# Relu kept in PSUM: convolution and gate read it there, and the order of the work is drawn anew

## The chip, the cores and the metric

One NeuronCore of a Trainium2 chip runs the whole program. The metric is the device time of one execution in microseconds, the median of a few runs. The engines are called TensorE (PE), VectorE (DVE), ScalarE (ACT), GpSimd (POOL) and SyncE (SP); the last issues nearly all DMAs.

## What is computed

Eight sequences of 576 positions go through causal attention with eight heads of 64, with a bias from a running sum, and then through a feed-forward block with a convolution of three taps over the positions:

```python
scores = where(causal, -1e9, q @ k.T / 8 + min(-(cum[i] - cum[j]), 0))
x = softmax(scores) @ v                       # 8 x 576 x 512
h = maximum(x @ w_in, 0)                      # 8 x 576 x 1024
conv_out[s] = cw[0]*h[s-1] + cw[1]*h[s] + cw[2]*h[s+1]
out = (h * sigmoid(conv_out)) @ w_out         # 8 x 576 x 512
```

All inputs and the output are fp32. The kernel keeps near fp32 accuracy by splitting operands into a high and a low part (`fp32r`) and summing three products.

## The kernel before

**Tiling.** The attention runs over 32 pairs of heads (`pair(p)`). For a pair TensorE forms scores (task `sh`, line L1106) of which VectorE takes the maximum of each row (`mx`, L1143, with the row sums `rw` added for pairs from 7 on), then the scores again transposed (`sc`, L1230), of which ScalarE takes a sigmoid in place of the exponential (L1247), then sums and the product with v (`sum` L1333, `pv` L1281). The block after it runs over eight batches, two halves of the positions (320 and 256 columns) and four pairs of 128 features: 64 groups, `moe_h(b, hf, fp)`. A group is 48 products into one PSUM pair (task `h`, L1446), the Relu (L1467, ScalarE), the middle tap (L1481 on ScalarE or L1483 on VectorE), two outer taps for each of its two feature blocks (L1496, VectorE), a sigmoid (L1510, ScalarE), the product with h (L1516, VectorE), and the split into `u` (L1525, L1530). The output products `o` (L1595) follow, and their copies (L1629) and stores.

**PSUM.** It is used as four tiles `ps0` to `ps3` of two banks each, here called pairs. A task that allocates one (`psb()`) keeps it until the last task that uses it is done. The Relu reads the pair and writes `ht` in SBUF, and the pair is free after it; the taps and the product read `ht`. A token `qh` lets two groups be between their first product and their Relu.

**The order.** A planner (`Sched.play`) plays the whole program once, while the program is built, with a fixed duration for each task, and writes the instructions out in the order in which its play started them. Each engine then takes its own instructions strictly in that order and waits where data or a buffer is missing. Among ready tasks the planner takes the one with the lowest due time, which is a formula plus a shift from the table `DUE`. It counts a DMA as landed `LAND` us (`LAND0` in the first 100 us) after its bytes have passed. Tasks marked as needing the SBUF port that VectorE shares with GpSimd (a third entry `True` in the options) are not started on both engines at once, and where one was made to wait, a dependency is added between them. Where TensorE would stand for more than 0.6 us (in the first 100 us, at all), and a PSUM pair is free, it is given a product of the mask that nobody reads (`stay_awake`, L1661). The row sums `rw` of a pair of heads come by one DMA (576 KB, L1055) into a single buffer.

Of the kernel before, what the change touches and what calls it, by code (L numbers as in the profile page):

```python
# [17 lines left out]
ALU = mybir.AluOpType  # L18
# [33 lines left out]
LAND = 0.85  # L52
NEAR = 0.2
LANES, RATE0, EARLY, LAND0 = 8, 300e3, 100.0, 1.2
# [41 lines left out]
    "pads":  # L96
        "0 -12.85 1 -220.76 2 -41.24",
    "ind":
# [396 lines left out]
def kernel(  # L495
# [928 lines left out]
    def h_tag(b, hf, f):  # L1424
        return at(HP * (b + 1)) + LAG + hf * HT + f * HT / NF

    def moe_h(b, hf, fp):
        u, ht, ct = buf("u"), buf("ht"), buf("ct")
        hw = HW[hf]
        k0 = hw - 2 * P  # L1430
        tg = h_tag(b, hf, 2 * fp)
# [307 lines left out]
```

## Time and profile before

| | us |
|---|---|
| median of 3 runs | 764.38 (763.74 to 765.69) |
| the profiled execution | 767.12 |
| its span, first to last instruction | 765.4 |
| TensorE busy in it | 733.4 |
| VectorE, ScalarE, GpSimd busy | 543.9, 406.2, 283.0 |
| mean granted TensorE clock | 0.993 |

Matmuls overlap each other, so the start of one row to the start of the next tells more of TensorE's pace than the length of a row. A row of a time line joins alike instructions (x24), and the bracket behind it tells how long the engine stood before it and what ended that.

### The profile page before, as it was taken

Reading aid. Unit: us, or ns where it says so; the run is one execution under the profiler, and the core shown is the slowest. Engines: PE = TensorE matmul, PEld = TensorE weight load, DVE = VectorE, ACT = ScalarE, POOL = GpSimd, SP = SyncE. Lnnn points to the kernel's source line nnn. Section 1 sums busy time; section 2 is a strip of 40 time slices with the busy share of each in tenths; the row PEclk is TensorE's granted clock in tenths of the full one; section 3 lists DMA queues with packets and bytes.
Section 4 is the critical chain, followed back from the end, with each engine's and each line's share of the span. In section 5 each row is a group of like instructions: output and inputs, shape, how many; then the busy total and the mean of one; then the engine's idle time right before and its main releaser. Section 6 shows DMA issues by size and latency. Waiting matters only on the chain.

```text
span 765.4 us, 24336 instructions
## 1 busy us (share of the span) xinstructions
PE 733.4 (96%) x10066; PEld 620.0 (81%) x10066; DVE 543.9 (71%) x1438; ACT 406.2 (53%) x714; POOL 283.0 (37%) x403
## 2 busy tenths in 40 slices
PE   7999999989999999899999899999899999999999
PEld 5787888879887788777888689777787887888997
DVE  7899997664967678785578848767875795756642
ACT  6566655465645356454655535545565454734441
POOL 5646420324143512536344262344157426311000
PEclk9999999989999999999999999999999999999999
DMA  7667532242333322334122443233323421101001
GB/s 224 207 190 219 155 90 85 69 130 64 97 94 114 99 77 71 107 100 143 51 89 65 125 157 85 79 125 99 100 63 101 115 85 59 45 18 45 28 30 43
DMA packets 50089, 75.50 MB, mean 99 GB/s; under 512 B 13690, under 2 KB 26298, under 8 KB 49978
## 3 DMA queue, kind: packets, MB, share of 16 engines
q1 hardware_dynamic: 49960, 73.92, 32.0%
q8 instruction: 79, 1.29, 0.7%
q14 instruction: 32, 0.26, 0.1%
q10 hardware_dynamic: 18, 0.02, 0.0%
HBM read 63.53 MB, written 10.03 MB: 96 GB/s over the span
## 4 chain that ended last, share of the span: by engine, by line
PE 57%; DVE 16%; DMA 12%; POOL 6%; issue 6%; ACT 3%; SPq 1%; POOLq 0%; DVEq 0%; ACTq 0%
PE ps L1595 19%; PE ps L1446 18%; PE ps L1230 9%; PE ps L1281 6%; DVE ps L1143 5%; DMA rw<-cum_d 4%; DVE ct L1496 3%; DMA rb<-ri_d 3%; PE ps L1333 2%; PE ps L1106 2%; POOL ad L1296 2%; DMA raw<-qk 2%; DVE r L1143 1%; POOL rw L1064 1%; POOL pt L1258 1%
## 5 line engine op out<-in xcount | busy, mean ns | idle before, releaser
L1446 PE MATMUL ps<-x,wi 64*128 64x258 f32 (+1 forms) x3072 | 228.5, 297 | 4.0 <-DVE r L1143 2.1
L1446 PEld LDWEIGHTS ps<-x,wi 64*128 64x128 f32 x3072 | 214.2, 187 | 11.0 <-DVE r L1143 2.6
L1595 PE MATMUL ps<-wo,u 64*128 64x512 f32 x1536 | 193.3, 393 | 0.7
L1143 DVE CUSTOM_DVE_ANT_0 ps<-ps,rw 128x448 f32<-128x448 f32 (+4 forms) x250 | 109.6, 439 | 97.7 <-POOL rw L1064 38.8
L1595 PEld LDWEIGHTS ps<-wo,u 64*128 64x128 f32 x1536 | 140.3, 185 | 29.0 <-ACTq L811 2.5
L1247 ACT ACTIVATE pt<-ps,less 128x1024 f32<-128x1024 f32 (+1 forms) x128 | 116.2, 925 | 28.6 <-PE ps L1230 24.3
L1496 DVE SCALAR_TENSOR_TENSOR ct<-ht,cw_sb,ct 128x320 f32<-128x320 f32 (+3 forms) x256 | 123.6, 524 | 9.7 <-POOL u L1530 4.6
L1064 POOL TENSOR_SCALAR_AFFINE_SELECT rw<-rw 128x256 f32<-128x256 f32 (+1 forms) x125 | 48.2, 393 | 206.8 <-DVE ct L1496 79.7
L1230 PE MATMUL ps<-s 64*128 64x288 f32 (+4 forms) x1152 | 109.3, 303 | 7.4 <-ACT pt L1247 3.1
L1230 PEld LDWEIGHTS ps<-s 64*128 64x128 f32 (+1 forms) x1152 | 82.8, 181 | 14.1 <-ACT pt L1247 4.8
L1281 PE MATMUL ps<-pt,v 128*32 128x448 f32 (+4 forms) x1536 | 92.8, 388 | 0.0
L1258 POOL TENSOR_SCALAR_AFFINE_SELECT pt<-pt 128x256 f32<-128x256 f32 (+1 forms) x115 | 43.5, 397 | 108.9 <-DVE ct L1496 41.4
L1281 PEld LDWEIGHTS ps<-pt,v 128*32 128x32 f32 x1536 | 50.6, 110 | 39.8 <-issue 29.9
L1467 ACT ACTIVATE ht<-ps 128x642 f32<-128x642 f32 (+1 forms) x64 | 41.8, 652 | 64.5 <-PE ps L1446 64.2
L1510 ACT ACTIVATE ct<-ct 128x640 f32<-128x640 f32 (+1 forms) x64 | 43.7, 683 | 43.3 <-DVE ct L1496 39.9
L1106 PE MATMUL ps<-s 64*128 64x288 f32 (+4 forms) x384 | 50.1, 319 | 9.1 <-DVE r L1143 7.2
L1516 DVE TENSOR_TENSOR ct<-ct,ht 128x640 f32<-128x640 f32 (+1 forms) x64 | 48.4, 756 | 9.0 <-ACT ct L1510 7.2
L1525 ACT CAST u<-ct 128x512 fp32r<-128x512 f32 x56 | 34.6, 618 | 30.9 <-DVE ct L1516 30.3
L1230 PE MATMUL ps<-eq,ek 64*128 64x288 f32 (+1 forms) x360 | 50.6, 301 | 0.0
L1481 ACT ACTIVATE ct<-ht,cw_sb 128x320 f32<-128x320 f32 (+1 forms) x95 | 47.7, 531 | 2.4
L1106 PEld LDWEIGHTS ps<-s 64*128 64x128 f32 x384 | 33.4, 189 | 18.7 <-DVE r L1143 10.5
L1143 DVE DVE_READ_ACCUMULATOR2_ANT r<- 128x1 f32 x314 | 44.4, 141 | 0.0
(120 smaller groups left out, 933.5 us busy)
## 6 DMA issues: line engine op xcount, KB each, us to landing
raw<-qk SPq DMA_DIRECT2D x32, 576.0 KB
rw<-cum_d SPq DMA_DIRECT2D x25, 576.0 KB
v<-vp SPq DMA_DIRECT2D x32, 320.0 KB
rb<-ri_d SPq DMA_DIRECT2D x64, 144.0 KB
out<-ob SPq DMA_DIRECT2D x32, 256.0 KB
w<-w_in SPq DMA_DIRECT2D x8, 512.0 KB
ht<-w_out SPq DMA_DIRECT2D x8, 256.0 KB
w<-w_out SPq DMA_DIRECT2D x4, 512.0 KB
```

The source lines that it names most:

```text
L1064: nc.gpsimd.affine_select(out=RW_t[:, :, o : o + k], in_=RW_t[:, :, d : d + k], pattern=[[0, 2], [-1, k]], compare_op=ALU.is_ge, fill=NEG, ...
L1106: nc.tensor.matmul(dst[j], l, m, start=(k == 0), stop=(k == 1 or late))
L1143: nc.vector.tensor_tensor_reduce(out=bank(pb, j, o, o + c1 - c0), in0=bank(pb, j, o, o + c1 - c0), in1=add_, scale=1.0, scalar=acc if c0 e ...
L1230: nc.tensor.matmul(d, l, m, start=(k < 2), stop=(k >= len(steps) - 2 or (t == L and k < 2)), skip_group_check=t == L,)
L1247: nc.scalar.activation(PT[:, :, o : o + w], both(pb, 0, w), AF.Sigmoid, bias=less, scale=0.125,)
L1258: nc.gpsimd.affine_select(out=reg, in_=reg, pattern=[[0, 2], [1, dg]], compare_op=ALU.is_ge, fill=0.0, base=0, channel_multiplier=-1,)
L1281: nc.tensor.matmul(bank(pvs, n, o0, o0 + c1 - c0)[gs], vt[0:jt, t, gs], PT_t[g // 2][0:jt, O_T[t] + c0 : O_T[t] + c1], start=(t == 0), sto ...
L1446: mm = nc.tensor.matmul(bank(hb, i, 0, XW[hf]), wi[rows[j], k_ // 2, c, f * P : f * P + P], x[rows[j]], start=not turned and k == 0, stop= ...
L1481: nc.scalar.activation(o, src, AF.Copy, scale=w)
L1496: nc.vector.scalar_tensor_tensor(cc[:, lo:hi], h_[:, sh + lo : sh + hi], cw_sb[:, 3 * f + k : 3 * f + k + 1], cc[:, lo:hi], op0=ALU.mult, ...
L1516: nc.vector.tensor_tensor(cc, cc, H_t[ht.slot][:, :, hf : hf + hw], op=ALU.mult)
L1595: mm = nc.tensor.matmul(bank(pb2 if m else pb, m, 0, cw_), l, r, start=turned + fp + n == 0, stop=turned == 1 and fp == FP - 1 and n == le ...
```

## The change

Three things are changed. The Relu writes back into the PSUM pair that it reads; `ht` is no longer allocated by a group. The middle tap, the outer taps and the product with h read the pair; the pair and the token `qh` stay with the group until that product is done. The outer taps of a group wait for both of its middle taps. These tasks no longer carry the mark of the shared port, and their planned durations are those below. `LAND` goes from 0.85 to 1.3, `LAND0` from 1.2 to 1.425. And every shift in `DUE` is another number.

```diff
-LAND = 0.85
+LAND = 1.3
-LANES, RATE0, EARLY, LAND0 = 8, 300e3, 100.0, 1.2
+LANES, RATE0, EARLY, LAND0 = 8, 300e3, 100.0, 1.425
...
     "h":
-        "0.0 -27.58 0.1 14.39 1.0 28.37 1.1 73.88 2.0 51.44 2.1 91.75 3.0 -156.77 3.1 71.3 "
+        "0.0 -347.28 0.1 -5.08 1.0 -98.9 1.1 -51.12 2.0 -60.78 2.1 268.69 3.0 -326.95 "
...
-        u, ht, ct = buf("u"), buf("ht"), buf("ct")
+        u, ct = buf("u"), buf("ct")
...
             nc.scalar.activation(
-                H_t[ht.slot][:, :, 0 : hw + 1], both(hb, hf, hf + hw + 1), AF.Relu
+                both(hb, hf, hf + hw + 1), both(hb, hf, hf + hw + 1), AF.Relu
             )
...
-                     uses=[hb, ht, q])
+                     uses=[hb, q])
+        t_cs = []
...
-                src = H_t[ht.slot][:, i, hf : hf + hw]
+                src = bank(hb, i, 2 * hf, 2 * hf + hw)
...
-            t_c = add(f"ce{b}.{hf}.{f}", [("ACT", 0.29 + hw / 1.2e3), ("DVE", 0.21 + hw / 1.92e3, True, 2.0)],
-                      [t_relu, t_cw], h_tag(b, hf, f) + 0.1, center, uses=[ht, ct])
-
-            t_tap = t_c
+            t_c = add(f"ce{b}.{hf}.{f}", [("ACT", 0.29 + hw / 1.2e3), ("DVE", 0.2 + hw / 0.96e3, False, 3.0)],
+                      [t_relu, t_cw], h_tag(b, hf, f) + 0.1, center, uses=[hb, ct])
+            t_cs.append(t_c)
+
+        for i in range(2):
+            f = 2 * fp + i
+            t_tap = t_cs
...
-                    h_ = H_t[ht.slot][:, i, :]
+                    h_ = bank(hb, i, hf, hf + hw + 1)
...
-                t_tap = add(f"t{'ab'[k // 2]}{b}.{hf}.{f}", [("DVE", 0.205 + hw / 0.96e3, True)], [t_tap],
-                            h_tag(b, hf, f) + 0.1, tap, uses=[ht, ct])
+                t_tap = add(f"t{'ab'[k // 2]}{b}.{hf}.{f}", [("DVE", 0.215 + hw / 0.96e3)], t_tap,
+                            h_tag(b, hf, f) + 0.1, tap, uses=[hb, ct])
...
-                cc, cc, H_t[ht.slot][:, :, hf : hf + hw], op=ALU.mult
+                cc, cc, both(hb, 2 * hf, 2 * hf + hw), op=ALU.mult
...
-        t_m = add(f"mu{b}.{hf}.{fp}", [("DVE", c_tt(2 * hw), True)], [t_g], tg, mul, uses=[ct, ht])
+        t_m = add(f"mu{b}.{hf}.{fp}", [("DVE", c_tt(2 * hw) + 0.03)], [t_g], tg, mul, uses=[ct, hb, q])
```

TensorE's order before, in the first half of batch 5: two groups (`x0`, `wi`) take turns in `ps0` and `ps1`, and the sums of a pair of heads (`pt`, `onehot`) go into `ps0`.

```order
L1595 MATMUL ps3_67<-wo_75,u0_1768 128x512 x12
L1446 MATMUL ps0_64<-x0_89,wi_74 128x322 x24
L1446 MATMUL ps1_65<-x0_89,wi_74 128x322 x24
L1446 MATMUL ps0_64<-x0_89,wi_74 128x322 x24
L1446 MATMUL ps1_65<-x0_89,wi_74 128x322 x24
L1333 MATMUL ps0_64<-pt_88,onehot_70 32x128
```

Between the last product of the group in `ps0` and the next writer of `ps0` stand 24 products. TensorE's order after, in the same half batch: a group in `ps3`, the scores of the next pair (`s1`), a group of the second half (`x1`) in `ps0`, and the sums into `ps3`.

```order
L1448 MATMUL ps3_67<-x0_89,wi_74 128x322 x24
L1108 MATMUL ps2_66<-s1_79 128x448 x2
L1108 MATMUL ps2_66<-s1_79 128x64 x2
L1448 MATMUL ps3_67<-x0_89,wi_74 128x322 x24
L1108 MATMUL ps1_65<-s1_79 128x320 x2
L1108 MATMUL ps1_65<-s1_79 128x192 x2
L1448 MATMUL ps0_64<-x1_90,wi_74 128x258 x48
L1335 MATMUL ps3_67<-pt_88,onehot_70 32x128
```

Now four score products and 48 products of the next group stand between the last product into `ps3` and its next writer, and that writer needs the whole gate of the group to be done. VectorE's order before, at two groups of the same half batch (`ct0` and `ct1` are their results, `ISA` is a row maximum and the read of its result):

```order
L1483 TENSOR_SCALAR ct0_103<-ht0_100,cw_sb_73 128x320
L1496 SCALAR_TENSOR_TENSOR ct0_103<-ht0_100,cw_sb_73,ct0_103 128x319 x2
L1496 SCALAR_TENSOR_TENSOR ct0_103<-ht0_100,cw_sb_73,ct0_103 128x320 x2
L1496 SCALAR_TENSOR_TENSOR ct1_104<-ht1_101,cw_sb_73,ct1_104 128x319 x2
L1496 SCALAR_TENSOR_TENSOR ct1_104<-ht1_101,cw_sb_73,ct1_104 128x320
L1516 TENSOR_TENSOR ct0_103<-ct0_103,ht0_100 128x640
```

VectorE's order after, at the group in `ps3` of the fence above:

```order
L1523 TENSOR_TENSOR ct2_105<-ct2_105,ps0_64 128x640
L1486 TENSOR_SCALAR ct0_103<-ps3_67,cw_sb_73 128x320
L1502 SCALAR_TENSOR_TENSOR ct0_103<-ps3_67,cw_sb_73,ct0_103 128x319 x2
L1502 SCALAR_TENSOR_TENSOR ct0_103<-ps3_67,cw_sb_73,ct0_103 128x320 x2
L1145 ISA ps2_66,r0_94<-ps2_66,rw_84 128x64
L1145 ISA r0_94 128x1
```

The taps read `ps3` in place of `ht0`, and row maxima of the next scores stand between them and the group's product (L1523). Over the whole program the order of TensorE has 228 products of the mask in place of 242; VectorE has 52 middle taps in place of 33, and GpSimd 50 subtractions for x in place of 20.

## Rows read from the trace of the kernel before

**Rows 1.** The page's first part: busy us, share of the span, instructions.

```profile
PE 733.4 (96%) x10066; PEld 620.0 (81%) x10066; DVE 543.9 (71%) x1438; ACT 406.2 (53%) x714; POOL 283.0 (37%) x403
```

**Rows 2.** TensorE's groups by line: count, busy us, mean ns, idle before, releasers.

```profile
L1661 PE MATMUL ps<-mask 128*128 128x256 bf16 x242 | 33.1, 284 | 4.5 <-POOL mask L678 2.2 <-ACT ht L1467 1.8 <-DVE r L1143 0.5
```

**Rows 3.** TensorE's waits: who waited for whom, us in total, times, longest.

```profile
PE ps L1106 <- DVE r L1143: 7.2, 7, 2.7
...
PE ps L1446 <- ACT ht L1467: 1.2, 2, 0.7
```

**Rows 4.** TensorE's time line at 156 us: start, length, instructions, wait before.

```profile
156.41 0.80 PE L1106 MATMUL ps<-s 64*128 64x448 f32 x4 [2.70 <-DVE r L1143]
```

**Rows 5.** Two stretches: length, busy PE, PEld, DVE, ACT, POOL, clock, DMA.

```profile
145.00:165.00 20.00, 17.30 (x255) 14.89 (x255) 12.33 (x33) 11.20 (x19) 8.08 (x9) 0.83 0.35 110
310.00:322.00 12.00, 9.96 (x112) 8.83 (x108) 8.46 (x26) 3.85 (x9) 6.75 (x12) 0.86 0.41 138
```

**Rows 6.** VectorE's and GpSimd's time lines at 150 and at 314 us.

```profile
150.37 2.87 DVE L1496 SCALAR_TENSOR_TENSOR ct<-ht,cw_sb,ct 128x255 f32<-128x255 f32 x1 [2.61 <-POOL rw L1064]
...
150.31 2.65 POOL L992 TENSOR_TENSOR s<-raw,s 128x1152 fp32r<-128x1152 f32 x1
...
314.52 0.47 DVE L1143 CUSTOM_DVE_ANT_0 ps<-ps,rw 128x288 f32<-128x288 f32 x1
...
314.48 1.47 POOL L1411 TENSOR_TENSOR x<-rb,x 128x322 fp32r<-128x322 f32 x2
```

**Rows 7.** Time lines of SyncE, VectorE and TensorE around 313 us.

```profile
308.45 0.39 SPq L1055 DMA_DIRECT2D rw<-cum_d  x1
...
313.96 0.47 DVE L1143 CUSTOM_DVE_ANT_0 ps<-ps,rw 128x288 f32<-128x288 f32 x1 [1.89 <-DMA rw<-cum_d]
...
315.10 0.50 PE L1106 MATMUL ps<-s 64*128 64x448 f32 x4 [1.99 <-DVE r L1143]
```

**Rows 8.** TensorE's time line at the first scores.

```profile
7.68 2.69 PE L1661 MATMUL ps<-mask 128*128 128x256 bf16 x23
...
11.45 0.40 PE L1106 MATMUL ps<-ek,eb 64*128 64x288 f32 x2 [0.75 <-ACT ek L1039]
```

**Rows 9.** Groups by line and shape on ScalarE and VectorE; last, VectorE's time line.

```profile
L1467 ACT ACTIVATE ht<-ps 128x642 f32<-128x642 f32 x32 | 22.6, 707 | 38.5 <-PE ps L1446 38.3
L1467 ACT ACTIVATE ht<-ps 128x514 f32<-128x514 f32 x32 | 19.1, 598 | 26.0 <-PE ps L1446 25.8
L1481 ACT ACTIVATE ct<-ht,cw_sb 128x320 f32<-128x320 f32 x48 | 25.1, 557 | 1.3
L1481 ACT ACTIVATE ct<-ht,cw_sb 128x256 f32<-128x256 f32 x47 | 22.6, 505 | 1.1
L1510 ACT ACTIVATE ct<-ct 128x640 f32<-128x640 f32 x32 | 23.6, 737 | 15.6 <-DVE ct L1496 12.3 <-PE ps L1595 1.8 <-PE ps L1230 1.4
L1510 ACT ACTIVATE ct<-ct 128x512 f32<-128x512 f32 x32 | 20.1, 629 | 27.6 <-DVE ct L1496 27.6
...
L1516 DVE TENSOR_TENSOR ct<-ct,ht 128x640 f32<-128x640 f32 x32 | 26.3, 822 | 3.9 <-ACT ct L1510 3.3 <-POOL rw L1064 0.6
L1516 DVE TENSOR_TENSOR ct<-ct,ht 128x512 f32<-128x512 f32 x32 | 22.1, 689 | 5.1 <-ACT ct L1510 3.9 <-POOL pt L1258 0.7 <-POOL rw L1064 0.5
L1496 DVE SCALAR_TENSOR_TENSOR ct<-ht,cw_sb,ct 128x320 f32<-128x320 f32 x64 | 33.4, 545 | 0.1
L1496 DVE SCALAR_TENSOR_TENSOR ct<-ht,cw_sb,ct 128x256 f32<-128x256 f32 x64 | 29.1, 477 | 2.7 <-POOL u L1530 2.1 <-ACT ct L1481 0.2
L1143 DVE CUSTOM_DVE_ANT_0 ps<-ps,rw 128x320 f32<-128x320 f32 x50 | 24.9, 499 | 13.3 <-POOL rw L1064 11.0 <-PE ps L1106 1.5
...
140.67 1.67 DVE L1496 SCALAR_TENSOR_TENSOR ct<-ht,cw_sb,ct 128x256 f32<-128x256 f32 x4
```

**Rows 10.** TensorE's time line at 137 us: 48 products of h, and the next row.

```profile
137.41 3.11 PE L1446 MATMUL ps<-x,wi 64*128 64x258 f32 x48
140.32 0.59 PE L1230 MATMUL ps<-s 64*128 64x288 f32 x6
```

More of the change, by code (lines that the diff above doesn't have):

```diff
@@ L91 @@
     "x":
[4 rows of a table removed]
[4 rows of a table added]
     "pads":
-        "0 -12.85 1 -220.76 2 -41.24",
+        "0 -135.98 1 -136.71 2 -132.38",
     "ind":
[1 row of a table removed]
[1 row of a table added]
     "cw":
[1 row of a table removed]
[1 row of a table added]
     "wi":
[3 rows of a table removed]
[3 rows of a table added]
     "wo":
[6 rows of a table removed]
[6 rows of a table added]
     "qk":
[9 rows of a table removed]
[9 rows of a table added]
     "hi":
[4 rows of a table removed]
[4 rows of a table added]
     "lo":
[4 rows of a table removed]
[4 rows of a table added]
     "dr":
[4 rows of a table removed]
[4 rows of a table added]
     "dp":
[1 row of a table removed]
[1 row of a table added]
     "dq":
[1 row of a table removed]
[1 row of a table added]
     "eq":
[4 rows of a table removed]
[4 rows of a table added]
     "sh":
[4 rows of a table removed]
[4 rows of a table added]
     "tn":
[4 rows of a table removed]
[4 rows of a table added]
     "sc":
[4 rows of a table removed]
[4 rows of a table added]
     "pv":
[4 rows of a table removed]
[4 rows of a table added]
     "nm":
[4 rows of a table removed]
[4 rows of a table added]
     "fo":
[4 rows of a table removed]
[4 rows of a table added]
     "vn":
[4 rows of a table removed]
[4 rows of a table added]
     "rw":
[3 rows of a table removed]
[3 rows of a table added]
     "rk":
[12 rows of a table removed]
[14 rows of a table added]
 }
@@ L1459, in moe_h @@
                        [x_done[b * HP + c] for c in range(NC)] + [t_wi[2 * fp], t_wi[2 * fp + 1]],
-                       h_tag(b, hf, 2 * fp + i), h_mm(i), alloc=[hb, u, ht, ct, q] if i == 0 else [],
+                       h_tag(b, hf, 2 * fp + i), h_mm(i), alloc=[hb, u, ct, q] if i == 0 else [],
                        uses=xs + ([hb] if i else []), mode="r")
@@ L1500, in tap @@
                     )
-                t_tap = add(f"t{'ab'[k // 2]}{b}.{hf}.{f}", [("DVE", 0.205 + hw / 0.96e3, True)], [t_tap],
-                            h_tag(b, hf, f) + 0.1, tap, uses=[ht, ct])
-            taps.append(t_tap)
+                t_tap = add(f"t{'ab'[k // 2]}{b}.{hf}.{f}", [("DVE", 0.215 + hw / 0.96e3)], t_tap,
+                            h_tag(b, hf, f) + 0.1, tap, uses=[hb, ct])
+                t_tap = [t_tap]
+            taps += t_tap
         tg = h_tag(b, hf, 2 * fp + 1) + 0.2
```

162 rows, old and new, of the table DUE are left out of this document.

## The prediction

> **What bounds the kernel now.** I read the page's first part, then TensorE's groups by line, then TensorE's waits, then the time lines around the longest of them. TensorE is busy 733.4 of 765.4 us; no other engine is over 71% [rows 1]. So the time is TensorE's own work plus whatever it waits for. Of its busy time 33.1 us is no work: 242 products of the mask (L1661) that the planner puts where it expects TensorE to stand still, so that the clock stays up [rows 2]. Idle (765.4 - 733.4 = 32.0) and filler together are 65 us, and that is all this change can move, because it alters no real product. The longest single entry among the waits is 7.2 us for a score product (L1106) that needs a PSUM pair which VectorE's row maxima (L1143) still hold [rows 3].
>
> Two of these waits are long and cost twice. At 153.7 us TensorE stands 2.70 us [rows 4], and the granted clock over 145 to 165 us is 0.83; at 313 us it stands 1.99 us [rows 7], and the clock over 310 to 322 is 0.86 [rows 5]. Missing clock is 0.17 x 20 = 3.4 us and 0.14 x 12 = 1.7 us. I read the fall as the follower of a wait near 2 us.
>
> **The change part by part.** The two orders differ nearly everywhere, so I price kinds of waits. The profiled execution took 767.12 us (765.4 of them span), 2.7 more than the median 764.38; I take the sum as a difference and put it on the median.
>
> *Fillers after 100 us.* The order before has 70 fillers there ahead of its last run, the order after 32. A filler is worth 2.69 / 23 = 0.117 us [rows 8], so 38 fewer give **-4.4 us** if they stand for wait that is gone. They may not: a filler needs a free PSUM pair, and the change keeps pairs longer, so a wait can stand there unfilled. Taken -4.1, bounds -4.4 and 0.
>
> *Fillers ahead of the first scores.* 64 instead of 46. In the trace these run until the first score product at 10.4, and the bias product behind it then waits 0.75 us for the key rows until 11.45 us [rows 8]. 18 x 0.117 = 2.1 us more would move both to 12.4, 1.0 later than now. Bounds 0 and +1.0; the other fillers up to 100 us change by 3. Taken **+0.7**.
>
> *Taps and the gate product read PSUM.* Before, both their inputs are in SBUF. At 150.37 us one tap took 2.87 us, in step with a subtraction on GpSimd that took 2.65 [rows 6]; four such taps otherwise take 1.67 [rows 9]. The maxima behind that tap are what TensorE waited for at 153.7. A VectorE operation with one input in PSUM did not stretch beside such subtractions: 0.47 us at 314.52, while two of GpSimd's ran from 314.48 to 315.95 [rows 6]. So the taps stop colliding. The price is that place: at most 2.70 + 3.4 = 6.1 us, at least 0 if another wait is next there. Taken **-4.0**. The tap's own length changes little: with one input in PSUM, 320 columns took 0.499 us in the maxima against 0.545 in the taps [rows 9], so -0.05 to +0.05 each; 256 x 0.05 = 13 us on an engine that is idle 221 us is covered except inside the chain below. The middle tap loses more on VectorE: the order has 52 there instead of 33. What the planner moves from VectorE to GpSimd (30 of the 64 subtractions of x, 26 of u and us) goes to an engine that is 37% busy; I cost it at nothing.
>
> *The planner's landing time.* It rises from 0.85 to 1.3 us. The load of the row sums, issued at 308.45, let the maxima go at 313.96, 5.5 us on, and TensorE waited 1.99 us [rows 7]. A later planned landing puts other work in front. This kind is 1.99 + 1.7 of clock there and at most what is left of the entry of 7.2 us without its two long waits, 7.2 - 2.7 - 2.0 = 2.5: 6.2 us. Bounds -6.2 and 0; taken **-3.0**, since 0.45 us is a small part of 5.5.
>
> *The pair is held longer.* This is what the change adds. Before, the pair of an h group comes free when the Relu has been written to SBUF; after, only when the gate product has been formed. What waits for it is the next product into that pair, and TensorE takes its instructions in order, so everything behind waits too. The chain of one group, on the rows of 256 columns: Relu 0.598, middle tap 0.505, four taps 1.67, sigmoid 0.629, product 0.689, together 4.09; for 320 columns 0.707 + 0.557 + 0.737 + 0.822, and the taps longer by 4 x (0.545 - 0.477), together 4.76 [rows 9]. Rounded up for the handovers, I estimate **4.2 and 4.8 us**. Against it stands the work that TensorE's order has between a group's last product and the next product into that pair. The order fences show two such places: before, 24 products lie between, after, 4 score products and 48 of h, whose 48 take 2.91 us [rows 10]. Over all groups, at the trace's pace, the median is 1.7 us before and 6.0 after; the planner allows for the longer hold. But eight places fall well short: 3.11, 3.18, 3.58 and 3.58 us against 4.2, and 3.13, 3.60, 3.63 and 4.51 against 4.8. Their shortfalls are 1.09 + 1.02 + 0.62 + 0.62 and 1.67 + 1.20 + 1.17 + 0.29, together 7.7 us. The same account for before (a chain of 0.7 to 0.8) gives 2 to 3 us, and the trace has 1.8 + 1.2 us of waits on the Relu [rows 2, 3], so it is of the right size. Net +4.7; with chains half a microsecond longer, some 11. Taken **+6**, because VectorE serves maxima between the taps. The Relu's write into PSUM has no row; I bound it by 0.598 -0.1 and +0.1 and see no weight in it.
>
> The Trainium skill speaks against this step: "PSUM — Partial Sum Buffer", under "Summary: rules for kernel authors", says to evacuate promptly because PSUM is tight. By that rule the last term decides, which is the first rival below. "ScalarE: Activation LUTs", under "Step-by-step: what each stage is for", says that ScalarE writes PSUM sooner than SBUF, but that this helps only where TensorE does not need most of PSUM; no row of before shows such a write.
>
> Sum: -4.1 + 0.7 - 4.0 - 3.0 + 6.0 = -4.4; 764.4 - 4.4 = **760.0 us**.
>
> **The rivals.** *A, slower: the held pair decides.* VectorE puts the maxima of four products between the steps of a chain, or the row load blocks it; then chains run 0.5 us longer, and the shortfalls give 14 - 3 = +11. Two of the waits exceed 2 us, and the clock falls as at 313 us, +1.7 each. The lock gives only -2, the landing 0: 764.4 - 4.1 + 0.7 - 2 + 11 + 3.4 = **773 us**. For it: in the trace VectorE waits for row loads in front of its maxima, so its queue does stand. Against: the planner has widened the distances. It decides from chains of about 5.2 us on.
>
> *B, no change.* TensorE's waits come from the row loads and their maxima; each moved wait comes back at the next load, and the fillers that went were unfilled waits: **764 us**. For it: the loads are the same 25, and no real work goes.
>
> *C, more gain.* Both long waits and their clock go entirely (6.1 + 3.7), the smaller ones of that entry too (2.5), the fillers with them (4.1), and the pair costs only 2: 764.4 - 16.4 + 0.7 + 2 = **751 us**.
>
> **How the numbers follow.** Forecast 0.42, A 0.24, B 0.10, C 0.24. A measurement here can tell 0.3% (2.3 us) from no change, so faster is under 762.1 and slower over 766.7. Of the forecast's own spread (755 to 765) about a fifth lies within 2.3 us of no change. Faster 0.33 + 0.24 = 0.57, same 0.09 + 0.10 = 0.19, slower 0.24. The range runs from a little under C to A, 748 to 773, which leaves about 0.1 on each side.
>
> **What would show it.** Right: no tap over 0.7 us; the clock at 1.0 from 30 us on; filler products 228 and idle after 100 us under 30 us; waits of TensorE on the gate product (the line of its multiplication) of 4 to 9 us in sum. Wrong: waits on the gate product over 12 us, or a clock under 0.95 in any stretch of 20 us, is A. If idle plus filler stays at 65 us with other names, it is B. If taps from PSUM take over 0.6 us, the chain was mis-sized.

## The result and the profile after

The changed kernel takes **756.04 us** (median of 8 runs, 753.07 to 758.32) against 764.19 for the kernel before (8 runs beside them, 760.13 to 767.81). The ratio is **0.989, with an interval of 0.986 to 0.992**: 8 us less, between 6 and 11. The forecast was 760.0, with a range of 748 to 773. The profiled execution of after took 753.07 us and is the fastest of its eight; that of before took 767.12, longer than seven of the eight. So the two spans, 765.4 and 751.3, lie 14.1 apart, and of what the traces show below only some 8 us stand for the usual run. Medians are of all executions; ratios leave out two single ones that took far longer than the rest, one of run 4's twelve (1148.51 us) and one of before (2432.51).

The page of after, its first part and the group of the mask products (the answer to [rows 1, 2]):

```profile
PE 730.9 (97%) x10052; PEld 616.2 (82%) x10052; DVE 536.1 (71%) x1404; ACT 392.1 (52%) x676; POOL 335.2 (45%) x466
...
L1668 PE MATMUL ps<-mask 128*128 128x256 bf16 x228 | 32.1, 291 | 2.8 <-POOL mask L680 2.7
```

TensorE is still what bounds. Its idle time is 751.3 - 730.9 = 20.4 us where it was 32.0. GpSimd does 52 us more, as the order said it would, and behind its first filler TensorE never waits for GpSimd. TensorE's waits of after: who waited for whom, us in total, times, longest (the answer to [rows 3]):

```profile
PE ps L1448 <- DVE ct L1523: 3.9, 5, 1.5
PE ps L1668 <- POOL mask L680: 2.7, 1, 2.7
PE ps L1108 <- ACT pt L1249: 1.6, 2, 0.9
PE ps L1232 <- DVE ct L1523: 1.3, 2, 0.9
PE ps L1335 <- DVE ct L1523: 0.9, 1, 0.9
PE ps L1108 <- DVE r L1145: 0.8, 2, 0.6
PE ps L1232 <- ACT pt L1249: 0.8, 2, 0.4
PE ps L1448 <- DVE r L1145: 0.8, 2, 0.6
PE ps L1108 <- DVE ct L1523: 0.7, 1, 0.7
```

The rows that end in L1523 are the new wait, a pair that the gate product has not yet given back: 3.9 + 1.3 + 0.9 + 0.7 = 6.8 us. The 7.2 us for the row maxima are 0.8. Summed over all rows of this view from 95 us to the last output products, the maxima fall from 10.7 to 2.2 us, the Relu from 3.0 to 0, everything else but the gate product from 9.1 to 2.0; with the new 6.8 the sum goes from 22.8 to 11.0.

The two stretches of [rows 5], after (length; busy PE, PEld, DVE, ACT, POOL; clock; DMA share; GB/s), and the groups of the changed steps by shape (busy us, mean ns; the answer to [rows 9]):

```profile
145.00:165.00 20.00, 19.93 (x350) 17.64 (x350) 15.71 (x48) 11.98 (x21) 6.30 (x9) 1.00 0.33 113
...
310.00:322.00 12.00, 12.00 (x154) 10.81 (x152) 8.41 (x21) 6.24 (x10) 4.92 (x10) 1.00 0.41 112
```

```profile
L1502 DVE SCALAR_TENSOR_TENSOR ct<-ps,cw_sb,ct 128x320 f32<-128x320 f32 x64 | 32.5, 540 | 0.0
L1502 DVE SCALAR_TENSOR_TENSOR ct<-ps,cw_sb,ct 128x256 f32<-128x256 f32 x64 | 27.9, 474 | 1.9 <-ACT ct L1484 1.9
L1523 DVE TENSOR_TENSOR ct<-ct,ps 128x640 f32<-128x640 f32 x32 | 26.1, 816 | 9.9 <-ACT ct L1517 9.9
L1469 ACT ACTIVATE ps<-ps 128x642 f32<-128x642 f32 x32 | 22.1, 691 | 42.5 <-PE ps L1448 41.4 <-ACT ob L1636 0.8 <-PE ps L1167 0.4
L1469 ACT ACTIVATE ps<-ps 128x514 f32<-128x514 f32 x32 | 18.7, 583 | 29.0 <-PE ps L1448 26.5 <-PE ps L1167 2.3
```

The clock is whole in both stretches, TensorE all but never stands there, and the outer taps and the product cost what they cost before (540 for 545 ns, 474 for 477, 816 for 822). No outer tap is over 550 ns. Only the middle tap on VectorE got longer, as the prediction said, 480 for 351 ns at 256 columns (before, then after):

```profile
L1483 DVE TENSOR_SCALAR ct<-ht,cw_sb 128x256 f32<-128x256 f32 x17 | 5.9, 351 | 9.0 <-ACT ht L1467 9.0
...
L1486 DVE TENSOR_SCALAR ct<-ps,cw_sb 128x256 f32<-128x256 f32 x27 | 12.6, 480 | 24.7 <-ACT ct L1484 20.3 <-PE ps L1232 2.2 <-ACT ps L1469 2.0
```

So it is not the steps that got shorter; the waits between them changed.

Behind the start, the longest wait of after is one for the gate product, at 328.58 us (time lines of ScalarE, VectorE and TensorE; the last bracket is the wait):

```profile
323.67 0.58 ACT L1469 ACTIVATE ps<-ps 128x514 f32<-128x514 f32 x1 [1.76 <-PE ps L1448]
...
327.04 0.35 DVE L1145 CUSTOM_DVE_ANT_0 ps<-ps,rw 128x192 f32<-128x192 f32 x1
...
329.34 0.68 DVE L1523 TENSOR_TENSOR ct<-ct,ps 128x512 f32<-128x512 f32 x1
...
330.07 1.11 PE L1448 MATMUL ps<-x,wi 64*128 64x258 f32 x14 [1.49 <-DVE ct L1523]
```

The chain of this group, from its Relu to the end of its product, took 330.02 - 323.67 = 6.35 us, with maxima (L1145) between its taps. Over the 64 groups its median is 5.2 us for 256 columns and 6.2 for 320, its least 4.44 and 5.25. At each of the nine places where TensorE waited for the gate product the chain was longer than the 4.2 and 4.8 us of the forecast, by 0.5 to 3.7 us.

### The profile page after: what moved, and what is told of

The parts are those of the page before. It is cut to its first block, busy times and chain, and to the rows that moved or that the text cites. A ratio compares the mean times of both kernels' runs of the same rounds, so it can differ in the third digit from the quotient of the medians.

```text
span 751.3 us, 24363 instructions
## 1 busy us (share of the span) xinstructions
PE 730.9 (97%) x10052; PEld 616.2 (82%) x10052; DVE 536.1 (71%) x1404; ACT 392.1 (52%) x676; POOL 335.2 (45%) x466
## 4 chain that ended last, share of the span: by engine, by line
PE 45%; DVE 9%; issue 3%; ACT 2%; POOL 2%; DMA 1%; POOLq 0%; ACTq 0%; DVEq 0%; SPq 0%
PE ps L1448 15%; PE ps L1602 15%; PE ps L1232 7%; PE ps L1283 5%; DVE ps L1145 3%; DVE ct L1502 2%; PE ps L1335 1%; PE ps L1108 1%; DVE r L1145 1%; DVE ct L1523 1%; PE ps L1668 1%; DMA rw<-cum_d 1%; DVE ct L1486 1%; ACT pt L1249 0%; POOL ad L1298 0%
## 5 line engine op out<-in xcount | busy, mean ns | idle before, releaser
L1602 PE MATMUL ps<-wo,u 64*128 64x512 f32 x1536 | 196.9, 394 | 0.9
L1145 DVE CUSTOM_DVE_ANT_0 ps<-ps,rw 128x448 f32<-128x448 f32 (+4 forms) x250 | 109.5, 439 | 46.1 <-POOL rw L1066 17.4
L1502 DVE SCALAR_TENSOR_TENSOR ct<-ps,cw_sb,ct 128x255 f32<-128x255 f32 (+3 forms) x256 | 115.9, 507 | 2.8 <-ACT ct L1484 2.7
L1232 PE MATMUL ps<-s 64*128 64x288 f32 (+4 forms) x1152 | 106.8, 299 | 2.8 <-DVE ct L1523 1.3
L1232 PEld LDWEIGHTS ps<-s 64*128 64x128 f32 (+1 forms) x1152 | 81.1, 177 | 9.3 <-ACT pt L1249 2.6
L1469 ACT ACTIVATE ps<-ps 128x642 f32<-128x642 f32 (+1 forms) x64 | 40.8, 637 | 71.5 <-PE ps L1448 67.9
L1523 DVE TENSOR_TENSOR ct<-ct,ps 128x640 f32<-128x640 f32 (+1 forms) x64 | 48.0, 751 | 18.6 <-ACT ct L1517 18.5
L1537 POOL TENSOR_TENSOR u<-ct,u 128x512 fp32r<-128x512 f32 x32 | 41.3, 1290 | 44.4 <-ACT u L1532 39.7
L1486 DVE TENSOR_SCALAR ct<-ps,cw_sb 128x256 f32<-128x256 f32 (+1 forms) x52 | 26.1, 513 | 47.6 <-ACT ct L1484 39.8
L1413 POOL TENSOR_TENSOR x<-rb,x 128x322 fp32r<-128x322 f32 (+1 forms) x50 | 37.7, 776 | 47.1 <-ACT x L1409 43.0
L1108 PE MATMUL ps<-s 64*128 64x288 f32 (+4 forms) x384 | 47.8, 307 | 5.2 <-ACT pt L1249 1.6
L1532 ACT CAST u<-ct 128x512 fp32r<-128x512 f32 x59 | 36.5, 618 | 25.8 <-DVE ct L1523 24.4
```

The source lines that it names most:

```text
L1108: nc.tensor.matmul(dst[j], l, m, start=(k == 0), stop=(k == 1 or late))
L1145: nc.vector.tensor_tensor_reduce(out=bank(pb, j, o, o + c1 - c0), in0=bank(pb, j, o, o + c1 - c0), in1=add_, scale=1.0, scalar=acc if c0 e ...
L1232: nc.tensor.matmul(d, l, m, start=(k < 2), stop=(k >= len(steps) - 2 or (t == L and k < 2)), skip_group_check=t == L,)
L1502: nc.vector.scalar_tensor_tensor(cc[:, lo:hi], h_[:, sh + lo : sh + hi], cw_sb[:, 3 * f + k : 3 * f + k + 1], cc[:, lo:hi], op0=ALU.mult, ...
L1523: nc.vector.tensor_tensor(cc, cc, both(hb, 2 * hf, 2 * hf + hw), op=ALU.mult)
L1602: mm = nc.tensor.matmul(bank(pb2 if m else pb, m, 0, cw_), l, r, start=turned + fp + n == 0, stop=turned == 1 and fp == FP - 1 and n == le ...
```

## The experiments

Ratios are to the kernel before, with their 95% interval; that of after is 0.989 (0.986 to 0.992).

**1. The same order, all in SBUF.** The Relu writes SBUF, and the three steps read it there; not an instruction changes its place.

```diff
-                both(hb, hf, hf + hw + 1), both(hb, hf, hf + hw + 1), AF.Relu
+                H_t[ct.slot][:, :, 0 : hw + 1], both(hb, hf, hf + hw + 1), AF.Relu
...
-                    h_ = bank(hb, i, hf, hf + hw + 1)
+                    h_ = H_t[ct.slot][:, i, :]
```

> The order of after, instruction for instruction, but the Relu writes SBUF again and the middle tap, the four taps and the gate product read there: the code of before in the order of after. Theory 1 (what pays is that the taps and products leave the shared port): the waits of TensorE on the gate product (6.8 us in after) go, but taps and products of VectorE stretch beside GpSimd's subtractions, which are busy 335 us here and are no longer kept apart from them; many taps over 0.7 us, some over 2; 760 to 775 us, slower than after (756.0). Theory 2 (what pays is the new order alone, and the held pair is a price): few stretched taps stand on the path, and the time is after minus the 6.8 us of waits, 749 to 752 us.

**2. The same order, taps in SBUF, pair held.** As 1, but the product takes its h out of the pair.

```diff
-            nc.vector.tensor_tensor(
-                cc, cc, both(hb, 2 * hf, 2 * hf + hw), op=ALU.mult
+            nc.vector.scalar_tensor_tensor(
+                cc, both(hb, 2 * hf, 2 * hf + hw), 0.0, cc, op0=ALU.max, op1=ALU.mult
             )
```

> The same order, Relu to SBUF, middle tap and taps read SBUF, but the gate product takes max(h, 0) out of the PSUM pair itself, so the pair is held as long as in after. Against the run with everything in SBUF it adds the hold alone (and one VectorE input per group that is no longer in SBUF). Theory 1 (the hold has its price): waits of TensorE on the gate product come back, 6 to 10 us in sum, and the time is 4 to 7 us over that of the run with everything in SBUF. Theory 2 (the order covers the hold): under 2 us between the two. Against after the rest is the taps' place: if taps in SBUF collide, this run is slower than after by 5 us or more; if not, within 2 us of after.

Measured: 799.84 us (ratio 1.049, 1.046 to 1.053) and 789.90 us (1.037, 1.034 to 1.040). Theory 1 had the direction of run 1, and its 760 to 775 was far too low. VectorE's taps and products, the first two rows of run 1 and the last two of run 2 (busy us, mean ns):

```profile
L1502 DVE SCALAR_TENSOR_TENSOR ct<-ht,cw_sb,ct 128x255 f32<-128x255 f32 (+3 forms) x256 | 149.5, 637 | 6.5 <-ACT ct L1484 6.2
L1523 DVE TENSOR_TENSOR ct<-ct,ht 128x640 f32<-128x640 f32 (+1 forms) x64 | 60.3, 943 | 17.7 <-ACT ct L1517 17.5
```

```profile
L1502 DVE SCALAR_TENSOR_TENSOR ct<-ht,cw_sb,ct 128x255 f32<-128x255 f32 (+3 forms) x256 | 151.7, 644 | 6.2 <-ACT ct L1484 5.8
L1523 DVE SCALAR_TENSOR_TENSOR ct<-ps,ct 128x640 f32<-128x640 f32 (+1 forms) x64 | 48.2, 754 | 18.1 <-ACT ct L1517 17.9
```

In after the same two groups have 115.9 and 48.0 us. What reads SBUF twice is stretched, what has an input in PSUM is not: in run 2 the product alone is back at 48.2. One place of run 1, VectorE's product, GpSimd's two subtractions and TensorE:

```profile
570.58 4.44 DVE L1523 TENSOR_TENSOR ct<-ct,ht 128x640 f32<-128x640 f32 x1 [1.09 <-ACT ct L1517]
...
569.62 2.10 POOL L1298 TENSOR_TENSOR ad<-pt 128x896 f32<-128x896 f32 x1
571.68 2.66 POOL L994 TENSOR_TENSOR s<-raw,s 128x1152 fp32r<-128x1152 f32 x1
...
576.07 0.76 PE L1108 MATMUL ps<-s 64*128 64x448 f32 x4 [2.42 <-DVE r L1145]
```

The product ends at 575.02, 0.68 us behind the end of the second subtraction (574.34): it stood through both, the maxima queued behind it, and TensorE waited 2.42 us for them. That is the picture of [rows 6], many times over: 34 of the 256 taps are over 0.7 us, in after none. The Trainium skill says under "Who interferes with whom" of "SBUF — State Buffer" that VectorE and GpSimd share a pair of ports as an exclusive lock, that a VectorE instruction with two SBUF inputs contends with a GpSimd one that reads SBUF, and that one with at most one SBUF input, outside its two-port modes, does not; these rows agree. Theory 2 fell: the order of after, without its code, is 37 us slower than before. Run 2 was expected over run 1 by the price of the hold and is 10 us under it, since its product also left the port; so these two don't give that price. They give the port's: 789.9 - 756.0, some 34 us, hang on the place of the Relu's result for taps and middle taps alone, in an order that no longer keeps GpSimd away from them.

**3. One group of 64.** Before's order on every engine; only the group with the tap of 2.87 us at 150.37 [rows 6] keeps its h in PSUM.

```diff
-                    h_ = H_t[ht.slot][:, i, :]
+                    h_ = bank(hb, i, hf, hf + hw + 1) if hb in inplace else H_t[ht.slot][:, i, :]
```

> Before's order on every engine, with one of the 64 channel groups changed as after has it: the one whose tap took 2.87 us at 150.37 us. Its Relu stays in PSUM in place, and its middle tap, four taps and gate product read there. Theory (that tap's collision is what stands behind TensorE's wait of 2.70 us and the clock of 0.83 behind it): no tap of the group is over 0.6 us, the gate product ends near 152.4 instead of 154.6, TensorE's longest wait there falls to 0.5 us (the next score product into that pair stands at 151.9), the clock over 145 to 165 us is 1.0, and the time is 3 to 6 us under before, 758 to 761. Rival (another wait is next at that place, or the clock falls anyway): within 1.5 us of before, 762.5 to 766.

Measured: 760.96 us, ratio 0.995 (0.992 to 0.998), by the ratio 3.7 us less than before. The stretch of [rows 5] and the time lines of VectorE, GpSimd and TensorE there:

```profile
145.00:165.00 20.00, 19.64 (x350) 16.70 (x348) 14.21 (x41) 15.57 (x25) 9.38 (x11) 1.00 0.46 141
```

```profile
148.65 0.48 DVE L1501 SCALAR_TENSOR_TENSOR ct<-ps,cw_sb,ct 128x255 f32<-128x255 f32 x1 [0.39 <-POOL rw L1064]
151.27 0.69 DVE L1522 TENSOR_TENSOR ct<-ct,ps 128x512 f32<-128x512 f32 x1 [2.14 <-POOL s L992]
...
148.58 2.65 POOL L992 TENSOR_TENSOR s<-raw,s 128x1152 fp32r<-128x1152 f32 x1
...
154.06 0.40 PE L1106 MATMUL ps<-s 64*128 64x448 f32 x3
```

The tap runs beside the same 2.65 us subtraction and takes 0.48. (The product still stood 2.14 us for that subtraction, since the order of before has it wait its turn at the port.) The score product has no wait, and the clock is 1.00. Since TensorE's order is the same product for product, the k-th of one trace can be set against the k-th of the other: at 150 us this run is 0.5 late, at 157 2.7 early, at 165 5.0 early. That is 5.5 us at this place, in this pair of traces. Theory held in the time and in every sign that it named.

Not all of the 5.5 us is the group's. Ahead of the subtraction GpSimd waits for the load of the row sums. It was issued at 143.92 us in before and at 144.00 here, and it let GpSimd go on 1.7 us sooner here, which nothing in this edit brings about (the first two rows are of before, the last is of this run):

```profile
149.69 0.65 POOL L1064 TENSOR_SCALAR_AFFINE_SELECT rw<-rw 128x256 f32<-128x256 f32 x2 [2.84 <-DMA rw<-cum_d]
...
154.00 0.69 DVE L1516 TENSOR_TENSOR ct<-ct,ht 128x512 f32<-128x512 f32 x1 [0.77 <-ACT ct L1510]
```

```profile
147.96 0.65 POOL L1064 TENSOR_SCALAR_AFFINE_SELECT rw<-rw 128x256 f32<-128x256 f32 x2 [0.61 <-DMA rw<-cum_d]
```

The gate product starts 2.7 us sooner than in before (151.27 for 154.00). Counted from the end of the subtraction (151.23 and 152.96), the group's change brings 1.0 of these. So what the group is worth is told by the ratio, 1.7 to 5.8 us, and not by the two traces.

**4. The pair held for one step more.** The order of after; the first product into a pair also waits for the rounding of u (L1532) in 56 of the 64 groups.

```diff
+            late[hb.slot] = copy_on(e)(moe_tiles["u"][u.slot][:, 0], C_t[ct.slot][:, :, k0:hw])
...
+                    tc.add_manual_dep(made[0], late.pop(b.slot).ins.name, data, reason="pair held longer")
```

> After, its order untouched, but the first product into a pair that a channel group held also waits for that group's next step, the rounding of u (0.65 us behind the gate product in the median), in the 56 places where the order allows it. Theory (the hold has a price at the ten places where TensorE waits for the gate product now, 6.8 us in sum): those waits grow by 10 x 0.65 = 6.5 us and a few new ones come up; the time is 5 to 9 us over after, 761 to 765. Rival (what waits for the gate product has slack behind it, the next wait takes it up): the waits grow and others shrink, under 3 us over after, below 759.

Measured: 763.05 us, ratio 0.998 (0.995 to 1.001), 7 us over after. Of TensorE's waits (lines are shifted by 2):

```profile
PE ps L1450 <- DVE ct L1525: 3.8, 5, 1.5
...
PE ps L1108 <- DVE vc L1389: 2.7, 1, 2.7
PE ps L1232 <- ACT u L1534: 2.3, 7, 0.6
PE ps L1232 <- DVE ct L1525: 1.3, 2, 0.9
PE ps L1108 <- ACT u L1534: 1.2, 3, 0.5
...
PE ps L1604 <- ACT u L1534: 0.6, 1, 0.6
PE ps L1232 <- DVE u L1534: 0.6, 1, 0.6
...
PE ps L1335 <- ACT u L1534: 0.4, 1, 0.4
```

The size is as the theory had it, but by chance, for the place is not. The nine waits on the gate product stay, with 6.7 us: they belong to 16 groups whose next product stands ahead of the rounding in the order, where nothing could be lengthened, so that of the 56 waits put in only 47 hold a pair longer. New waits of 5.1 us in sum stand at the rounding, in 13 places of those other groups. Product for product the run is 3.2 us behind after at 100 us, before any pair is held, and 9.7 at 740: 6.5 for the hold. So 0.65 us more on each of 47 holds, some 31 us together, costs 6.5: at 13 places the order has less slack than that, at the others it shows no wait, and the pair's price is real. The Trainium skill's rule to evacuate promptly ("PSUM — Partial Sum Buffer", "Summary: rules for kernel authors") is borne out by this run and contradicted by run 1: where evacuating means that the readers go to the shared port, it cost more than holding.

**5. The mask products.** Run 5a is after without the last 16 of the 64 ahead of the first score, run 5b without the 32 between 100 and 740 us, run 5c without the 32 behind the last output product. The edit is the same, with other counts:

```diff
+    woken = []
+
     def stay_awake(slot):
+        woken.append(slot)
+        if 48 < len(woken) <= 64:
+            return
```

> After without the last 16 of the 64 fillers ahead of the first score product. Theory (the fillers delay the head): the first score product starts at 11.1 us instead of 13.0, the first bias product waits for the key rows until 12.3 instead of 13.2, and everything behind is 0.9 us earlier: 755.1 us. Rival (the head's delay is taken up by a later load): the first softmax product at 34.1 us as now, 756 us. If missing fillers let the granted clock fall ahead of 30 us, 757 us or more.

> After without the 32 fillers between 100 and 740 us (3.8 us of TensorE). Theory (a filler stands where TensorE would wait anyway): idle time rises by 3 to 4 us, the time stays within 1 us of after, 755 to 757. Rival 1 (a filler is work in the way): 2 to 4 us faster, 752 to 754. Rival 2 (they keep the clock up): the run of 17 at 435.6 becomes a wait of 2 us, the granted clock falls below 0.95 behind it, and the time is 1.5 to 3 us longer, 758 to 759.

> After without the 32 fillers behind the last output product (746.5 to 750.2 us). The last store is issued at 747.3 to 748.1. Theory (the store's landing ends the program, not the fillers): within 0.5 us of after, 755.5 to 756.5. Rival (the fillers end it): 0.7 to 1.5 us faster, 754.5 to 755.3.

Measured: 5a 760.30 us (0.995, 0.992 to 0.997), 5b 755.62 (0.992, 0.989 to 0.995), 5c 756.05 (0.989, 0.985 to 0.993). 5b and 5c can't be told from after: what went as filler came back as idle time. Part 1 of 5b's page:

```profile
PE 725.8 (96%) x10020; PEld 612.3 (81%) x10020; DVE 536.5 (71%) x1404; ACT 392.1 (52%) x676; POOL 332.4 (44%) x466
```

5.1 us less busy than after in a span 1.6 longer, and those 1.6 came up ahead of 100 us; from there to 740 the two run level to 0.2 us. Its clock is 1.00 throughout. 5a missed, on the side of its last case, and its interval meets that of after at 0.992. The profiled execution (762.93 us) is the slowest of its twelve. In it the first bias product was 0.65 us earlier than in after, and 3.5 us were lost by 20 us. Its windows and TensorE's two long waits:

```profile
10.00:20.00 10.00, 8.01 (x58) 5.02 (x56) 7.44 (x15) 3.32 (x5) 5.14 (x4) 0.68 0.80 238
20.00:30.00 10.00, 10.00 (x93) 6.69 (x92) 8.48 (x20) 3.15 (x8) 4.25 (x3) 0.81 0.53 164
30.00:95.00 65.00, 60.01 (x1019) 47.71 (x1022) 52.62 (x105) 37.97 (x66) 36.45 (x31) 0.95 0.57 172
```

```profile
12.56 0.40 PE L1108 MATMUL ps<-ek,eb 64*128 64x288 f32 x2 [1.79 <-DMA ek<-grid_d]
...
59.44 0.63 PE L1108 MATMUL ps<-s 64*128 64x320 f32 x2 [3.94 <-DVE vc L1389]
```

In after the clock is 1.00 in all three. The 16 fillers covered a wait of 1.8 us for the key rows, and behind that wait the clock fell, to 0.68 over 10 to 20 us. The second wait, of 3.94 us, costs another 5.4 us in this trace, and that is not the fillers': run 4, which has them all, waits 2.7 us at the same product (the second row of its fence). The twelve executions fall into two halves: six with a mean clock of 0.995 or more took 755.0 to 759.8 us, six at 0.987 to 0.991 took 760.8 to 762.9. So 3.5 us at their own place are shown for these fillers, in the slowest execution; how the 4 us between the medians divide was not shown.

**6. Other numbers for the planner.** Five runs change one of the planner's numbers, or all, and let it plan anew: 6a after with `LAND` at 0.85, 6b before with `LAND` at 1.3, 6c after's code with all of before's numbers, 6d after with 1.31 in place of 1.30, 6e before with 0.86 in place of 0.85.

```diff
-LAND = 1.3
+LAND = 1.31
```

> After's code and table of due shifts, with the planned landing time of transfers behind 100 us back at 0.85 us. The order is planned anew, so all waits move. Theory (the landing time puts other work in front of the loads of the row sums): the waits of VectorE's maxima on the row load go from 4.8 us back towards the 19.4 of before, some of it reaches TensorE, 758 to 765 us. Rival (the landing time is not it): these waits stay under 8 us.

> Before's code and table, with only the planned landing time of transfers behind 100 us raised from 0.85 to 1.3 us. The order is planned anew. Theory: the waits of VectorE's maxima on the row load fall from 19.4 us to under 10, and what TensorE waits for the maxima falls from 7.2; 758 to 764 us if nothing else got worse. Rival: a table of due shifts that was chosen for another landing time is worth more than the landing time, and the time is 5 us or more over before, 769 or longer.

> After's code (Relu, taps and gate product in PSUM, the planner without the port for them and with the longer hold), with all of before's numbers: due shifts and both landing times. Theory 1 (the code brings the gain, the numbers polish it): within 5 us of after, 751 to 761 us. Theory 2 (the numbers are worth nothing without the code that they were chosen for): 10 us or more over before, 774 or longer.

> After with the planned landing time of transfers behind 100 us at 1.31 instead of 1.30 us, all else as it is. The order is planned anew and comes out different from a fifth of the way on. Theory (the table of due shifts was chosen by replays for exactly these numbers, and the choice is worth more than the change): 780 to 810 us, as the other orders that nobody chose. Rival (the order is good because of what the code allows): within 5 us of after, 751 to 761.

> Before with the planned landing time at 0.86 instead of 0.85 us, all else as it is: what the code of before does in an order that was not chosen. If an order in PSUM is better whatever the choice, this run is slower than the same step on after by some 10 us; if the choice is all, the two are alike, both 780 to 815 us.

Measured: 6a 793.45 us (1.038, 1.032 to 1.044), 6b 804.57 (1.053, 1.045 to 1.060), 6c 848.54 (1.109, 1.100 to 1.118), 6d 780.75 (1.021, 1.015 to 1.027), 6e 831.59 (1.088, 1.081 to 1.096). A step of 0.01 us costs 25 us on one kernel and 67 on the other. In 6a the maxima's wait for the row load is 22.8 us where after has 4.8, in 6b it is 16.1 where before has 19.4; but with all else moved too, that is no measure of the landing time by itself, which stays open. What the runs do say: orders planned from other numbers cost 781, 793 and 849 us with the new code, 805 and 832 with the old. That a table of shifts fits its code and its other numbers is worth several times the whole change, on either kernel. How the two tables were found, no run here shows. Before's order could not simply have been given the new code: with every instruction in its old place, only 18 of the 64 groups can be held in PSUM, since in the others the gate product stands behind work that itself waits for the pair.

## Why the prediction was right, and where it was not

The sign came out, and the time within 4 us of the forecast, though the gain of 8 us is nearly twice the 4.4 forecast; 756.0 lies about midway between the forecast and rival C's 751. The signs named beforehand came too: no outer tap over 0.55 us, a clock of 1.00 from 30 us on in the profiled run, 228 fillers, 15 us of idle time after 100 us, 6.8 us of waits on the gate product. Idle time and fillers together went from 65 to 52.5 us, which speaks against rival B. In part the size is luck, as the terms show.

*Taps read PSUM, taken -4.0 (0 to -6.1).* Right. Run 3 shows it alone: -3.7 us in the ratio, and no wait came next at its place. The 2.70 us from which the term was priced are in part the wait for a row load, which came 1.7 us later in that execution than in run 3's; that -4.0 and -3.7 agree so well is in part luck. What the term missed is that this place is only the part that the old order suffered. The old planner kept the port free; the new order does not, and in it the tiles' place is worth 44 us (run 1 against after). That freedom, and not one stretched tap, is what the new order uses: GpSimd took 52 us more work, and the maxima no longer stand behind stretched taps.

*The pair held longer, taken +6 (+4.7 to +11).* Right in kind; its size came out near only because two errors stand against each other. The trace has 6.8 us of waits on the gate product, in nine places, against the Relu's 3.0 that went: net 3.8, under the lower bound. The chains were mis-sized: 5.2 and 6.2 us in the median against 4.2 and 4.8, since VectorE serves maxima between the taps, as the text feared, and by the term's own account half a microsecond more was to cost some 11. The distances were mis-sized the other way. With chains as forecast, eight of the nine waits would not be there, because the chain's excess is longer than the wait, and 0.3 us would be left of the nine where the account had 7.7 in eight places. So TensorE had more work between than the account said. Rival A was to decide from chains of 5.2 us on. Both medians reach that, and it did not decide: the planner's distances leave room for most of the long chains. Run 4 shows what more would cost, 6.5 us for 0.65 on each of 47 holds.

*Fillers after 100 us, taken -4.1.* They went, 38 of them, and did not come back as idle time, which fell as well. But run 5b shows that a filler is worth nothing of itself. The term held as a count of waits that were gone, and it was no cause.

*Fillers ahead of the first scores, taken +0.7.* Wrong in its step, and outside its bounds. The head of after is later, by 1.8 us at the first bias product and 2.4 at the first product of h in the profiled runs. Of the 1.8, some 0.8 are that the key rows come later in the new order (12.2 us, not 11.4), which the term left out. The other 1.0 is the fillers', which run on past the key rows to 13.2. But taking fillers out does not give that back: without 16 of them, in run 5a, the bias product came 0.65 us sooner and the median was 4 us longer.

*Landing time, taken -3.0.* The waits it spoke of are gone: at 310 to 322 TensorE is never idle, and the clock is 1.00. Whether the landing time did it was not shown; part of its price was clock, and in run 3 a wait of 1.87 us at that place was followed by no fall at all.

*What the sum left out.* The waits on other work, 9.1 us before and 2.0 after, had no term. That is more than the 3.8 us between the forecast and the result, and the head's 2.4 stand against it; two traces that lie 14.1 apart don't divide 8.2 any finer. Nor can the gain be divided between code and choice of order: after's order without its code takes 800 us, and before's order can't carry the code.

## What to carry to other kernels

Before taking a tile off PSUM at once, ask what its readers will do in SBUF: with two SBUF inputs each stands in GpSimd's way, and here holding the bank for 5 to 6 us was cheaper than that. When an order was planned for certain durations, compare a code change only in an order planned for it, or in one left as it was with the change at a single place; a plan made anew from slightly other numbers differed by 25 us and more for no reason of the change. When two traces are compared at one place, look first whether a load landed at the same time in both. And fillers on an idle TensorE were no cost to be saved here; ahead of a wait of 1.8 us they paid for themselves in clock.

## What the runs showed of the hardware

A VectorE instruction with two SBUF inputs that met two GpSimd instructions back to back was stretched over both: 4.44 us instead of 0.82, up to 0.68 us behind the end of the second (run 1). With one of the two inputs in PSUM a tap took 0.48 us beside a subtraction of 2.65 (run 3), where it had taken 2.87 (before).

The clock fell behind idle times of TensorE of 2.70 and 1.99 us (before) and 1.79 (run 5a, to 0.68 over 10 to 20 us), and stayed at 1.00 behind 1.87 (run 3), 1.77 (run 5b) and 1.49 (after). It fell behind 1.79 us and not behind 1.87, so the length of the wait alone does not tell it; and the same kernel's runs differ in it: of after's eight, those at a mean clock of 0.995 took 757.3 to 758.3 us, those at 1.000 753.1 to 755.0.

The Relu written to PSUM took 691 and 583 ns where the same one to SBUF took 707 and 598. The Trainium skill's "ScalarE: Activation LUTs" ("Step-by-step: what each stage is for") has ScalarE write PSUM sooner; here that is 15 to 16 ns a group.
